# Transposes moved into the token loop, one engine per bank, and the guess products moved into the last pool of layer A

## The chip, the cores and the metric

The kernel runs on one core of one Trainium2 chip. The metric is the device time of the kernel in microseconds (us), as the median of several executions. Every execution has a profile summary with its span and the mean clock that the throttle granted to the matmul engine (PE).

Engine names in the profile: PE is the matmul engine, PEld its weight loads, DVE the vector engine, ACT the scalar engine, POOL the third elementwise engine, SP the engine that issues most DMAs. A transpose is a PE product with the identity. Products are written to a buffer called PSUM; a "bank" is one of its parts, and a "pool" is the kernel's reservation of tiles in it.

## The reference, cut to what matters

```python
x = A_x                                    # (1, 2048, 640), bf16
x = x + A(layernorm(x))                    # A: rfft2, times W, irfft2
x = x + B(layernorm(x), mem0, Wq, Wk, Wv, Wo)
x = x + A(layernorm(x))
x = x + B(layernorm(x), mem0, Wq, Wk, Wv, Wo)

def B(x, mem, ...):                        # 64 segments of 32 tokens, 32 heads of 128
    for s in range(64):
        h = concat(mem, x[segment s])      # 8 memory rows, then 32 tokens
        q, k, v = h @ Wq, h @ Wk, h @ Wv
        o = softmax(mask(q @ k.T * scale)) @ v @ Wo
        mem, out = o[:8], o[8:]
```

The recurrence over `mem` is not run segment by segment. The kernel guesses all memories at once from the segments' mean rows (mean rows times `Wv`, then times `Wo`), computes all segments in parallel, and checks the guess. That guess is what "guess products" means below.

The passage from A to B occurs twice. There, the last step of A yields normalized rows with tokens on the partitions, and B needs them transposed, with features on the partitions (`hT`), before its first query (q), key (k) and value products.

## The kernel before

The last step of layer A is a loop over 16 row tiles of 128 rows. `spectrum_d` and `tokens` are 6 + 6 products for a tile. `norm` normalizes two tiles. `add_u` adds a tile's rows to the segment sums.

```python
# Layer A, tokens(): the end of A
with tc.manual_schedule(engines={PE, ACT, DVE}):          # order as written
    for s0 in range(16 + 5):
        if s0 < 16:
            spectrum_d(s0)                 # psg, copied to Gs by ACT
        if 1 <= s0 <= 16:
            tokens(s0 - 1)                 # psy, copied to x by ACT, statistics on DVE
        if s0 >= 2 and s0 % 2 == 1 and s0 < 18:
            norm((s0 - 3) // 2)            # Ln, Exp on ACT; 4 tiny ops and 2 scalings on DVE
        if handoff is not None:
            if s0 < 10:
                handoff.wv_piece(s0)       # DMA of Wv
            if s0 >= 5:
                handoff.add_u(pp, xna[:, s0 - 5, :], s0 - 5)   # 5 small products
if handoff is not None:
    handoff.finish(pp)                     # segment means u
pp.release()                               # the last PSUM pool of A ends
if handoff is not None:
    handoff.transpose_all(xna)

# BStart.transpose_all: 80 transposes, in PSUM pools of their own
for c in range(5):
    ps = pt.tile([128, 16, 128], BF16, name="pstr", tag="pstr")     # two banks
    for s0 in range(16):
        nc.tensor.transpose(out=ps[:, s0, :], in_=xna[:, s0, c * 128:(c + 1) * 128], identity=ident[:])
    for g_ in range(4):
        dst = ...                          # 480 columns of hT
        src = ps[:, :, 2 * GS * g_:2 * GS * (g_ + 1)].rearrange("p s (w j) -> p w j s", j=2)
        (nc.vector.tensor_copy if g_ % 2 == 0 else nc.scalar.copy)(out=dst, in_=src)
    ...                                    # four smaller copies, also on both engines

# layer B, head 0, in PSUM pool pj
guess[0](pj, vb)                           # 160 products of 64 columns: Wv times u
q_x(w, 0)
q_x(w, 1)
guess[1](pj, vb)                           # 160 more: through Wo; cast; scatter into hT
...                                        # then the k products, which read those columns
```

## Time and profile before

| | before |
|---|---|
| median of 4 runs | 1654.55 us (1652.97 to 1655.66) |
| profiled span, mean granted PE clock | 1658.3 us, 0.987 |
| PE busy | 1563.1 us, 94% |
| first q product after the loop's start, passage 1 / 2 | 56.0 / 56.0 us |
| first k product after the loop's start, passage 1 / 2 | 72.3 / 72.3 us |

These are from the page of the kernel before: the busy time of each engine, and the chain of waits that ended last, by engine. PE is nearly always busy, and the work that follows one piece on the other is PE's.

```profile
PE 1563.1 (94%) x14240; PEld 1081.0 (65%) x14241; DVE 790.0 (48%) x2300; ACT 835.6 (50%) x2528; POOL 282.4 (17%) x206
...
PE 41%; DVE 2%; DMA 2%; ACT 1%; issue 0%; SPq 0%; DVEq 0%; ACTq 0%
```

So there is little to gain on average, but the passage is not average. This is the view by stretches of the kernel before, for the loop, the tail up to the first q product, and the two q heads with the second guess. The columns are the stretch (from:to), its length, then the busy time of PE, PEld, DVE, ACT and POOL with their instructions in brackets, the granted PE clock, the DMA share and GB/s.

```profile
94.00:122.90 28.90, 28.68 (x257) 20.57 (x256) 23.02 (x79) 23.40 (x44) 1.46 (x2) 1.00 0.91 321
122.90:150.00 27.10, 15.56 (x266) 14.86 (x267) 13.23 (x51) 10.29 (x30) 0.00 (x0) 0.75 0.40 120
150.00:166.30 16.30, 14.87 (x235) 10.16 (x232) 0.95 (x5) 5.62 (x13) 0.00 (x0) 1.00 0.01 2
```

The loop is PE-bound (28.68 of 28.90). The tail is not: PE works 15.56 of 27.10 us, and at a mean clock of 0.75. This is PE's timeline of that tail. The columns are start, duration, engine, line, operation, output<-input, shapes and count; in square brackets stands how long PE had been idle before, and for whom. Consecutive equal instructions are one line.

```profile
124.88 0.68 PE L1191 MATMUL psu<-sel,A1tok_S 128*128 128x64 bf16 x10 [2.20 <-DVE A1tok_S L120]
128.11 0.81 PE L1191 MATMUL psu<-sel,A1tok_S 128*128 128x64 bf16 x10 [2.55 <-DVE A1tok_S L120]
129.90 0.27 PE L1200 MATMUL psm<-ident,m 8*128 8x8 bf16 x5 [0.98 <-ACT u L1231]
130.10 4.38 PE L1206 MATMUL pstr<-ident,A1tok_S 128*128 128x128 bf16 x48
136.98 3.47 PE L1206 MATMUL pstr<-ident,A1tok_S 128*128 128x128 bf16 x32 [2.49 <-DVE B1hT_S L1218]
143.94 6.20 PE L1248 MATMUL psvb<-u,B1wv_S 128*128 128x64 bf16 x160 [3.49 <-DVE B1hT_S L1218]
149.98 4.56 PE L865 MATMUL psq<-B1hT_S,bB_S 128*128 128x480 bf16 x25
...
159.99 5.29 PE L1255 MATMUL psg<-bB_S,Wo_sb 128*128 128x64 bf16 x160 [0.21 <-ACT bB_S L867]
166.32 0.37 PE L846 MATMUL psk<-B1hT_S,bB_S 128*128 128x502 bf16 x1 [1.04 <-DVE B1hT_S L1225]
```

Read it downwards. PE waits 2.20 and 2.55 us for the last normalized rows. It transposes 48 tiles, waits 2.49 us for a two-bank tile to be emptied, transposes 32 more, and waits 3.49 us for the last copies, because the guess products stand in a new pool that takes over those banks. Before the first k product it waits 1.04 us for the scattered guess.

The copies that it waits for are these; the timeline of DVE and ACT in the second passage, first tile.

```profile
944.42 0.66 DVE L1211 COPY B2hT_S<-pstr 128x480 bf16<-128x480 bf16 x1 [1.49 <-PE pstr L1206]
945.17 0.56 ACT L1211 COPY B2hT_S<-pstr 128x480 bf16<-128x480 bf16 x1 [2.81 <-DVE B2hT_S L1211]
```

ACT starts at 945.17, after DVE ended at 945.08, and its releaser is DVE's copy. Both read the same banks. The Trainium skill, page "PSUM — Partial Sum Buffer", section "PSUM bank collisions raise a hardware error", says why: two engines may not touch one bank (and quadrant of partitions) at the same time, reads included, so such accesses have to be ordered. The trace agrees: two engines together emptied a tile no faster than one after the other.

### The profile page before, as it was taken

To read this page: it belongs to the slowest core of one execution; us is meant where nothing else is said; L and a number is where in the kernel's file an instruction comes from. 1 tells how busy PE (TensorE), PEld (TensorE's weight loads), DVE (VectorE), ACT (ScalarE), POOL (GpSimd) and SP (SyncE) were. 2 spreads that over 40 slices of the span, in tenths; PEclk is the share of its full clock that TensorE was granted. 3 is DMA by queue.
4 is the path that set the end of the run, shared out by engine and by line. 5 is a ranking of instruction groups with operands and counts; after the bars stand their busy time and mean duration, and the time that the engine had idled before them with its cause. 6 is when DMAs were issued, how large, how long until landed. Compare 5 with 4: busy or idle time off the path is not lost. (4 is left out here: it accounts for less than half of the span.)

```text
span 1658.3 us, 36195 instructions
## 1 busy us (share of the span) xinstructions
PE 1563.1 (94%) x14240; PEld 1081.0 (65%) x14241; DVE 790.0 (48%) x2300; ACT 835.6 (50%) x2528; POOL 282.4 (17%) x206
## 2 busy tenths in 40 slices
PE   4887999999999999899988789999999999999998
PEld 2566666666666666677755666666666666666775
DVE  5772455555545554543356724545545454544110
ACT  5373566666666666511114636666666666663000
POOL 0810112121211111100026002121211111111000
PEclk9998999999999999999999899999999999999999
DMA  4472143434434343633302703434344343436241
GB/s 155 156 274 72 53 148 132 155 117 148 136 138 144 130 154 127 233 125 96 96 13 88 260 2 110 160 116 150 132 142 137 133 156 127 140 130 226 68 127 54
DMA packets 167873, 218.05 MB, mean 131 GB/s; under 512 B 7374, under 2 KB 141836, under 8 KB 159756
## 3 DMA queue, kind: packets, MB, share of 16 engines
q1 hardware_dynamic: 167084, 213.34, 38.5%
q8 instruction: 113, 1.85, 0.4%
q0 software_dynamic: 608, 2.30, 0.4%
q14 instruction: 68, 0.56, 0.1%
HBM read 170.52 MB, written 45.09 MB: 130 GB/s over the span
## 5 line engine op out<-in xcount | busy, mean ns | idle before, releaser
L846 PEld LDWEIGHTS <-bB_S 128*128 128x128 bf16 x3180 | 260.2, 97 | 185.9 <-issue 6.6
L990 DVE TENSOR_TENSOR bB_S<-pso,bB_S 128x480 bf16<-128x480 f32 (+1 forms) x320 | 189.4, 592 | 266.3 <-PE pso L981 249.4
L925 ACT ACTIVATE bB_S<-pss 128x269 bf16<-128x269 f32 (+5 forms) x576 | 213.3, 385 | 191.7 <-PE pss L922 177.2
L1140 PE MATMUL psx<-Wo_sb,bB_S 128*128 128x320 bf16 x2048 | 288.2, 299 | 3.9 <-DMA bB_S<-oTx_d 3.9
L1140 PEld LDWEIGHTS <-bB_S 128*128 128x128 bf16 x2048 | 197.2, 98 | 80.5 <-DMA bB_S<-oTx_d 4.6
L905 DVE CAST bB_S<-psk 128x495 bf16<-128x495 f32 (+3 forms) x320 | 191.3, 598 | 115.0 <-PE psk L846 84.8
L950 POOL TENSOR_TENSOR bB_S<-bB_S,bB_S 128x634 f32<-128x634 f32 x64 | 99.2, 1550 | 820.9 <-ACT bB_S L946 809.9
L926 DVE TENSOR_TENSOR bB_S<-bB_S,maskf 128x269 bf16<-128x269 bf16 (+5 forms) x576 | 162.9, 287 | 152.9 <-ACT bB_S L925 149.2
L914 ACT CAST bB_S<-psv 128x512 bf16<-128x512 f32 (+1 forms) x288 | 160.5, 557 | 83.8 <-PE psv L912 83.4
L890 ACT ACTIVATE bB_S<-psq 128x480 bf16<-128x480 f32 x300 | 152.5, 508 | 97.9 <-PE psq L846 97.9
L846 PE MATMUL psk<-B2hT_S,bB_S 128*128 128x495 bf16 (+3 forms) x800 | 165.0, 342 | 2.6 <-DVE bB_S L905 1.4
L846 PE MATMUL psk<-B1hT_S,bB_S 128*128 128x495 bf16 (+3 forms) x800 | 165.0, 342 | 1.7 <-DVE B1hT_S L1225 1.2
L912 PE MATMUL psv<-bB_S,B1hT_S 128*128 128x256 bf16 x1360 | 163.4, 272 | 0.2 <-DVE bB_S L905 0.2
L912 PE MATMUL psv<-bB_S,B2hT_S 128*128 128x256 bf16 x1360 | 163.4, 272 | 0.2 <-DVE bB_S L905 0.2
L922 PEld LDWEIGHTS <-bB_S 128*128 128x128 bf16 x1216 | 103.1, 98 | 90.1 <-issue 6.3
L846 PE MATMUL psq<-B2hT_S,bB_S 128*128 128x495 bf16 (+5 forms) x780 | 157.6, 336 | 0.1
L846 PE MATMUL psq<-B1hT_S,bB_S 128*128 128x495 bf16 (+5 forms) x780 | 157.5, 336 | 0.1
L922 PE MATMUL pss<-bB_S 128*128 128x132 bf16 (+8 forms) x1216 | 148.4, 216 | 3.0
L912 PEld LDWEIGHTS <-B1hT_S 128*128 128x128 bf16 x1360 | 128.7, 98 | 13.7 <-issue 0.3
L912 PEld LDWEIGHTS <-B2hT_S 128*128 128x128 bf16 x1360 | 128.6, 98 | 13.7 <-issue 0.3
L981 PE MATMUL pso<-bB_S,bB_S 128*128 128x132 bf16 (+8 forms) x1216 | 119.6, 216 | 0.0
L981 PEld LDWEIGHTS <-bB_S 128*128 128x128 bf16 x1216 | 91.2, 98 | 15.7 <-DVE oTmf L991 0.5
(225 smaller groups left out, 1555.1 us busy)
## 6 DMA issues: line engine op xcount, KB each, us to landing
bB_S<-Rd SPq DMA_DIRECT2D x62, 1059.5 KB
oTx_d<-bB_S SPq DMA_DIRECT2D x60, 512.0 KB
bB_S<-oTx_d SPq DMA_DIRECT2D x56, 512.0 KB
bB_S<-in_B_Wq_dram SPq DMA_DIRECT2D x32, 320.0 KB
bB_S<-in_B_Wk_dram SPq DMA_DIRECT2D x32, 320.0 KB
bB_S<-in_B_Wv_dram SPq DMA_DIRECT2D x32, 320.0 KB
bB_S<-oTx_d SPq DMA_DIRECT2D x14, 384.0 KB
Wo_sb<-in_B_Wo_dram SPq DMA_DIRECT2D x4, 1280.0 KB
```

The lines of the kernel that those rows point to most:

```text
L846: nc.tensor.matmul(ps, lhsT=w[:, ch, hh * 128:(hh + 1) * 128], rhs=src[:, ch, lo:hi], start=(ch == 0), stop=(ch == 4))
L890: nc.scalar.mul(out=qv[:, :, 0:SEG], in_=x_view(ps, o, n)[:, :, 1:SW], mul=scale)
L905: nc.vector.tensor_copy(out=KTs[h % 2][:, lo:hi], in_=ps[:, 0:hi - lo])
L912: nc.tensor.matmul(ps[:, i * 256:(i + 1) * 256], lhsT=hT[:, ch, (t + i) * 128:(t + i + 1) * 128], rhs=w["Wv"][:, ch, :], start=(ch == 0), ...
L914: nc.scalar.copy(out=V[:, t:t + n, :].rearrange("p a b -> p (a b)"), in_=ps[:, 0:n * 256])
L922: nc.tensor.matmul(ps[:, off - o0:off - o0 + hi - lo], lhsT=KT[:, t * 128:(t + 1) * 128], rhs=QT[:, lo:hi], start=True, stop=True)
L925: nc.scalar.activation(out=E[:, 0:n], in_=ps[:, 0:n], func=ACTF.Exp)
L926: nc.vector.tensor_tensor(out=P[:, o0:o0 + n], in0=E[:, 0:n], in1=bs.mask[:, o0:o0 + n], op=ALU.mult)
L950: nc.gpsimd.tensor_tensor(out=accS, in0=accS, in1=sums_sb, op=ALU.add)
L981: nc.tensor.matmul(pso[:, lo - q0:hi - q0], lhsT=V[:, t, (h % 2) * 128:(h % 2 + 1) * 128], rhs=P[:, off:off + hi - lo], start=(i == 0), st ...
L990: nc.vector.tensor_tensor(out=oT.rearrange("p (r s j) -> p r s j", r=16, j=2)[:, :, s0:s0 + ns, :], in0=byclass(po), in1=rx, op=ALU.mult)
L1140: self.tc.nc.tensor.matmul(ps[:, 0:320], lhsT=lhs(h, k // 2), rhs=self.g["Wo_sb"][:, h, c0:c0 + 320], start=(h == 0), stop=(h == H - 1))
```

## The change

Its intent: begin transposing while the loop still runs, in tiles of one bank each that a single engine empties, and fill the rest of the tail with fewer things to wait for.

- A transposed tile now holds two feature blocks of four row tiles (8 transposes, one bank). 48 of the 80 transposes stand in the loop, at iterations 8, 9, 10, 12, 13, 14 and 16; 32 stay in the tail.
- Each such bank is emptied by DVE or by ACT alone. For one copy to serve four groups of columns, the columns of `hT` get a uniform pitch of 512: the function `hcol` shifts columns from 512 on by 7, so the groups then start at odd columns (7, 519, ...).
- The small sum products leave the loop for the tail, where PE would wait.
- The four tiny operations of each norm go from DVE to POOL (in the loop).
- The first guess products run within the last pool of A; the second guess stands between the q products of heads 0 and 1.

The diff, cut to its core (helpers, renames and the split of the norm into two functions are left out):

```diff
         with tc.manual_schedule(...):
-            for s0 in range(16 + 5):
-                ...                                   # as shown above
-        if handoff is not None:
-            handoff.finish(pp)
+            moved, late = [], []
+            for i in range(16 + 1):
+                for f in moved:
+                    f()
+                moved = []
+                if late:
+                    late.pop(0)()
+                if i >= 5 and i % 2 == 1:
+                    norm((i - 5) // 2)                # now only the scalings, DVE
+                if i >= 2:
+                    stats(i - 2)
+                if i < 16:
+                    spectrum_d(i)
+                if 1 <= i <= 16:
+                    tokens(i - 1)
+                ...                                   # rest of late
+                if i >= 4 and i % 2 == 0:
+                    inverse((i - 4) // 2, nc.gpsimd)  # Ln, Exp on ACT; tiny ops on POOL
+                ...                                   # pieces of Wv, memory rows
+                if i >= 8 and i % 4 < 3:
+                    n = i % 4
+                    jobs = handoff.rows_out(handoff.rows_in(pp, xna, i // 4 - 2, 2 * n), n != 1 and i < 16)
+                    ...                               # jobs: the copies, done an iteration later
+            stats(15)
+            norm(6)
+            for s0 in range(14):
+                handoff.add_u(pp, xna[:, s0, :], s0)
+            big = handoff.big(pp)
+            inverse(7, nc.vector)
+            handoff.do(moved)
+            second = handoff.rows_in(pp, xna, 2, 2)
+            norm(7)
+            for s0 in (14, 15):
+                handoff.add_u(pp, xna[:, s0, :], s0)
+            handoff.finish(pp)
+            handoff.do(handoff.rows_out(second, False))
+            pairs = [handoff.rows_in(pp, xna, 3, 2 * n, ps=big[:, 2 * n:2 * n + 2]) for n in range(2)]
+            ones = [handoff.rows_in(pp, xna, q, 4) for q in (2, 3)]
+            for job, on_dve in ((pairs[0], True), (pairs[1], False), (ones[0], True), (ones[1], True)):
+                handoff.do(handoff.rows_out(job, on_dve))
+            handoff.guess1(pp)
         pp.release()
-        if handoff is not None:
-            handoff.transpose_all(xna)
 ...
+    def hcol(self, k):
+        return k + (self.PRE if k >= 512 else 0)      # PRE = 7
 ...
                 if h == 0:
-                    guess[0](pj, vb)
                     q_x(w, 0)
+                    env["guess"](pj, bs.vb)
                     q_x(w, 1)
-                    guess[1](pj, vb)
```

## The prediction

> **What bounds the kernel now.** The page gives PE 94% of the 1658.3 us span, 0.987 mean clock; the chain of waits is PE work in layer B (value, key, query and output products). The change leaves those alone. It touches the passage from layer A to B, which occurs twice (PE clock 0.73 there).
>
> From the timeline of the second passage (us):
> - 906.4 to 934.9: token loop. PE-bound: 12 matmuls make 1.65 per row tile, 1.80 once the five small sum products ride along. Engine table by stretches (907 to 935.5): PE 28.1 of 28.5, ACT 23.6, DVE 23.2.
> - 934.9 to 941.3: the last norms (two DVE statistics groups, two Ln/Exp, eight tiny DVE operations, four scalings); PE waits 2.2 + 2.6.
> - 941.3 to 956.3: 80 transposes (48 in 4.4, 32 in 3.5, at half clock) with waits of about 1.0, 2.5 and 3.5. Each bank pair is read by DVE (0.65) and ACT (0.56) alternately, and the timeline shows each starting only after the other ended. The Trainium skill's page "PSUM — Partial Sum Buffer", section "PSUM bank collisions raise a hardware error", explains the ordering: two engines may not touch one bank at once.
> - 956.3 to 962.4: guess products, 6.2.
> - 962.4 on: q products of heads 0 and 1 (5.0 each), guess products through Wo (5.3), then 1.0 to 1.2 idle until DVE's cast and scatter let the k products start.
>
> **What the change does, per passage.**
> Removed from the tail: 48 of 80 transposes and their evictions go into the loop; the alternation of engines ends; fewer copies per transpose (group pitch made uniform); the pool boundary between transposes and guess products disappears; four tiny DVE operations per norm go to POOL.
> Added to the loop: 48 transposes at full clock, 48 x 0.056 = 2.7; minus 11.5 sum-product groups of 0.15, -1.7. ACT gets 2 x 0.56 + about 0.2 at two iterations, DVE about 2.4 per four iterations: DVE then has about 8.4 against PE's 7.7 per four iterations, ACT about 7.5. So I expect lag and waits of PE for normalized rows or Gs copies: 1.5 to 2.5. Loop: +2.5 to +3.5.
> Tail, from the last token product: ACT copy 0.85, statistics 1.1, lag 0.7, norm(6) behind POOL 0.9, Ln/Exp and small operations 1.5, scaling 0.8 (PE resumes at about 5 instead of 6), sums and 24 transposes 2 to 3, guess products 5.3 to 6.2: q products start at about 14 instead of 27.4: -13.
> Second guess before q of head 1: cast and scatter hidden, -1.2.
> Net about -11 per passage (all estimates from the durations above), -22 in all. Practically all of it is on the critical path, since PE is idle or cold there.
>
> DMA is saturated (share about 0.95) until 946; weights of heads 0 and 1 land shortly after. I expect them in time.
> Odd column starts of hT: the trace already has odd-start weights and moving rows (back products in A) at 0.098 and full rate, so no loss.
>
> **Prediction:** 1632 us, range 1626 to 1639. Faster by over 2%: 4%; within 2%: 95%; slower: 1%.
>
> **Right if** the profile shows: first q product of each passage 10 to 12 us earlier relative to the loop's start; transposes at about 0.06 in the loop; loop 31 to 32.5 us long; k products following q of head 1 without the 1 us gap; layer B's middle unchanged to 1 us.
>
> **Wrong if** PE waits for DVE or POOL inside the loop much longer (slow tiny POOL operations delay norms; gain shrinks by 3 to 6); the first weights land late because the queue is shared with stores; weight loads from odd columns slow (2720 of them); or the tail overlaps better than summed (gain to 28).

## The result, and the profile after

| | before | after |
|---|---|---|
| median of 4 runs | 1654.55 us | 1635.12 us (1632.62 to 1636.59) |
| ratio, with its 95% interval | | 0.9882 (0.9865 to 0.9899) |
| profiled span, granted clock | 1658.3 us, 0.987 | 1632.3 us, 0.994 |
| first q product after the loop's start | 56.0 / 56.0 us | 44.8 / 45.6 us |
| first k product after the loop's start | 72.3 / 72.3 us | 59.5 / 60.2 us |

A ratio is always the mean time of one kernel's runs over that of the other's of the same rounds, so it is not quite the ratio of the medians quoted. The interval says that the change is faster by 1.0 to 1.4%. All outputs are right.

The page of the kernel after: the same number of products, POOL with 70 more instructions, DVE with 58 fewer.

```profile
PE 1556.5 (95%) x14240; PEld 1071.8 (66%) x14241; DVE 780.6 (48%) x2242; ACT 837.0 (51%) x2520; POOL 294.8 (18%) x276
```

The stretches of the first passage of the kernel after, as before: loop, tail, the two q heads with the second guess.

```profile
93.60:124.20 30.60, 29.92 (x239) 21.16 (x238) 21.40 (x62) 25.86 (x50) 7.09 (x32) 1.00 0.84 302
124.20:138.50 14.30, 10.71 (x284) 9.72 (x285) 9.66 (x39) 8.89 (x21) 1.00 (x5) 1.00 0.77 232
138.50:153.10 14.60, 14.18 (x230) 9.60 (x230) 1.48 (x6) 4.86 (x12) 0.00 (x0) 1.00 0.01 2
```

The loop is 1.7 us longer: PE works 1.24 more and is idle 0.68 instead of 0.22. The tail is 12.8 shorter, and its clock is 1.00 instead of 0.75. The last stretch is 1.7 shorter. In the tail PE's idle time fell from 11.5 us (27.10 - 15.56) to 3.6 (14.30 - 10.71), and its busy time by 4.9.

PE's timeline of the kernel after: one batch of eight transposes inside the loop, then the end of the loop and the tail.

```profile
107.99 0.61 PE L1291 MATMUL pstr<-ident,A1tok_S 128*128 128x128 bf16 x8
108.44 1.00 PE L412 MATMUL psg<-A1gt_S,A1UT_S 128*128 128x321 bf16 x6
...
124.69 0.81 PE L1291 MATMUL pstr<-ident,A1tok_S 128*128 128x128 bf16 x6 [0.49 <-DVE A1tok_S L127]
125.64 1.92 PE L1254 MATMUL psu<-sel,A1tok_S 128*128 128x64 bf16 x60
128.38 0.68 PE L1254 MATMUL psu<-sel,A1tok_S 128*128 128x64 bf16 x10 [0.82 <-DVE A1tok_S L127]
...
130.48 1.06 PE L1291 MATMUL pstrb<-ident,A1tok_S 128*128 128x128 bf16 x16
...
132.69 0.38 PE L1291 MATMUL pstr<-ident,A1tok_S 128*128 128x128 bf16 x4 [0.93 <-ACT B1hT_S L1310]
132.91 4.87 PE L1274 MATMUL psvb<-u,B1wv_S 128*128 128x64 bf16 x160
138.46 4.54 PE L931 MATMUL psq<-B1hT_S,bB_S 128*128 128x480 bf16 x25 [0.67 <-ACT bB_S L1276]
143.45 4.83 PE L1338 MATMUL psg<-bB_S,Wo_sb 128*128 128x64 bf16 x160 [0.21 <-ACT bB_S L933]
...
153.10 4.66 PE L912 MATMUL psk<-B1hT_S,bB_S 128*128 128x502 bf16 x25 [0.21 <-ACT bB_S L933]
```

In the loop eight transposes took 0.45 us (107.99 to 108.44), 0.056 each; in the tail before, at a mean granted clock of 0.63 (half clock but for the last 1.1 us), 48 took 4.4 us, 0.09 each. Where PE waited 2.55 us for rows it now runs the 60 postponed sums and then waits 0.82. The guess products follow the last transpose without a wait (3.49 before), and k follows q after 0.21 (1.04 before).

The copies now overlap, because they read different banks; the timeline of DVE and ACT in the loop of the kernel after.

```profile
118.39 1.32 DVE L1306 COPY B1hT_S<-pstr 128x480 bf16<-128x480 bf16 x2
...
119.23 0.77 ACT L1306 COPY B1hT_S<-pstr 128x480 bf16<-128x480 bf16 x1
```

DVE's two copies last from 118.39 to 119.71 and ACT's begins at 119.23.

Outside the passage one group changed. These are the 495-column k products of the first layer B, of the kernel before and of the kernel after, in the view of groups by form (busy us and mean ns of one after the bar).

```profile
L846 PE MATMUL psk<-B1hT_S,bB_S 128*128 128x495 bf16 x320 | 75.9, 372 | 0.0
```

```profile
L912 PE MATMUL psk<-B1hT_S,bB_S 128*128 128x495 bf16 x320 | 76.2, 373 | 0.0
```

One nanosecond each is little, but there are some 2500 products of this kind. From the first to the last of the heads' stores that the trace lets one time (the stores `Rd<-bB_S`, the first to the fourth from the end), layer B took 458.72 us before and 459.61 after in the first layer, and 459.92 and 461.01 in the second: 0.9 and 1.1 us were given back (1.0 and 0.8 between the first and the last store `oTx_d<-bB_S`).

**The sum.** In the profiles the passages give -12.8 and -12.1 (loop's start to first k), the heads +2.0, and the way from the first k to the first store -0.3 each: -23.5 us. The median of the first pairing says -19.4 and the profiled spans say -26.0. The experiments below say which is nearer.

### The profile page after: what moved, and what is told of

The parts are those of the page before. It is cut to its first block, busy times and chain, and to the rows that moved or that the text cites. A ratio compares the mean times of both kernels' runs of the same rounds, so it can differ in the third digit from the quotient of the medians.

```text
span 1632.3 us, 36236 instructions
## 1 busy us (share of the span) xinstructions
PE 1556.5 (95%) x14240; PEld 1071.8 (66%) x14241; DVE 780.6 (48%) x2242; ACT 837.0 (51%) x2520; POOL 294.8 (18%) x276
## 3 DMA queue, kind: packets, MB, share of 16 engines
q1 hardware_dynamic: 167084, 213.34, 39.1%
```

## The experiments

Two calls of four kernels (e7, e2, e3, e4; then e0, e1, e5, e8), one of three (e6, e9, e10) and one of e11 alone, each call on one chip together with the kernel before; compare within a call where a few tenths of a per cent matter. "Mean" is the mean of the runs of those rounds.

| run | what | median us | ratio to before (95%) | mean, before in the same rounds |
|---|---|---|---|---|
| e7_before_again | the kernel before, again | 1656.39 | 0.9992 (0.9978 to 1.0005) | 1656.64 for before |
| e2_swap_only | before, second guess earlier | 1654.1 | 0.9988 (0.9974 to 1.0001) | 1654.64, 1656.64 |
| e3_one_engine | before, one engine per tile | 1649.64 | 0.9965 (0.9951 to 0.9978) | 1650.4, 1656.64 |
| e4_all_in_tail | after, no transposes in the loop | 1648.98 | 0.9949 (0.9936 to 0.9963) | 1649.12, 1656.64 |
| e0_after_again | the kernel after, again | 1633.16 | 0.9856 (0.9836 to 0.9876) | 1633.22, 1656.25 |
| e1_even | after, even columns | 1631.18 | 0.9851 (0.9836 to 0.9866) | 1631.4, 1656.25 |
| e5_inverse_dve | after, tiny operations on DVE | 1635.67 | 0.9877 (0.9862 to 0.9892) | 1635.95, 1656.25 |
| e8_even_u_late | e1, one copy before the means | 1630.53 | 0.9842 (0.9828 to 0.9855) | 1630.25, 1656.25 |
| e6_guess_outside | after, first guess in B's pool | 1636.73 | 0.9881 (0.9863 to 0.99) | 1636.19, 1655.87 |
| e9_stats_first | after, statistics before scaling | 1629.76 | 0.9846 (0.9827 to 0.9866) | 1630.32, 1655.87 |
| e10_best | e8 and e9 and two last tiles | 1629.5 | 0.984 (0.982 to 0.986) | 1629.28, 1655.87 |
| e11_even_stats_first | e1 and e9 | 1629.06 | 0.9849 (0.9826 to 0.9872) | 1629.76, 1655.38 |

And in the traces, from the start of the token loop to the start of the last transpose (passage 1) and of the first q and k products (passage 1 / 2):

| run | last transpose | first q | first k |
|---|---|---|---|
| before | 46.2 | 56.0 / 56.0 | 72.3 / 72.3 |
| e7_before_again | 46.0 | 56.6 / 55.6 | 73.0 / 72.0 |
| e2_swap_only | 46.1 | 55.8 / 55.7 | 71.0 / 70.8 |
| e3_one_engine | 43.3 | 52.1 / 52.2 | 68.5 / 68.6 |
| e4_all_in_tail | 47.0 | 53.5 / 53.2 | 68.2 / 67.8 |
| after | 39.2 | 44.8 / 45.6 | 59.5 / 60.2 |
| e0_after_again | 39.2 | 44.8 / 46.6 | 59.5 / 62.7 |
| e1_even | 39.3 | 45.0 / 45.9 | 59.7 / 60.6 |
| e5_inverse_dve | 40.5 | 46.1 / 46.3 | 60.7 / 61.0 |
| e6_guess_outside | 39.2 | 46.3 / 47.8 | 60.9 / 62.5 |
| e8_even_u_late | 38.4 | 45.0 / 46.3 | 59.7 / 60.9 |
| e9_stats_first | 38.5 | 44.1 / 45.0 | 58.8 / 59.7 |
| e10_best | 38.5 | 44.7 / 44.7 | 59.4 / 59.4 |
| e11_even_stats_first | 39.1 | 44.8 / 45.7 | 59.5 / 60.4 |

### How far do equal kernels differ? e7_before_again and e0_after_again

No edit: the kernel before and the kernel after, again.

> Control: the kernel before, unchanged, against itself. The profiled spans of before and after differ by 26.0 us, the medians of the runs by 19.4. Theory: the first profiled run of before (1660 us) was a run with some us more of cold clock or waits than usual, and this one shows a span near 1653 to 1656 us and a ratio of 1.000 within 0.2%. Rival: the passages really gain 25 us and something else loses 5; then this span is 1658 to 1660 again.

> Control for the next three: the kernel after, unchanged, on their chip. Expected 1633 to 1637 us, ratio 0.987 to 0.990, and pairs of heads in layer B 32.86 us apart as in its first profile (before: 32.80).

The kernel before against itself gave 0.9992, with 1 inside the interval. Its five spans were 1657.8, 1654.6, 1651.9, 1653.4 and 1654.8 us at granted clocks of 0.987, 0.990, 0.990, 0.989 and 0.989. The kernel after gave 1633.4, 1634.7, 1628.3 and 1629.4 at 0.995, 0.994, 0.998 and 0.998. The longer runs are those with the lower clock, so a single run is uncertain by some 3 us either way, and the three estimates of the gain (19.4, 23.0 here by the means, 26.0 by the profiles) do not contradict each other. The sum of 23.5 from the landmarks agrees with the 23.0. Single landmarks scatter too. Equal kernels agree to 0.3 us at the last transpose, but in two traces of the kernel before the first q differs by up to 0.6, with stretches of half clock of different length, and in two traces of the kernel after, in the second passage, by 1.0 and the first k by 2.5. There a pause of PE of varying length stands before them (see "What stays open"). So the first passage and the last transpose are the better measures.

### Is it the place of the transposes or how they are emptied? e4_all_in_tail and e3_one_engine

The theory: most of the gain comes from the transposes' place in the loop, where PE does them at full clock while it is busy anyway. The rival: what counts is that two engines no longer take turns on a bank, wherever the transposes stand.

```diff
 # e4_all_in_tail, on the kernel after
-                if i >= 8 and i % 4 < 3:
+                if False:
 ...
-                second = handoff.rows_in(pp, xna, 2, 2)
 ...
-                handoff.do(handoff.rows_out(second, False))
+                n_job = 0
+                for q in range(3):
+                    for n in range(3):
+                        if (q, n) != (2, 2):
+                            handoff.do(handoff.rows_out(handoff.rows_in(pp, xna, q, 2 * n), n_job % 2 == 0))
+                            n_job += 1
```

```diff
 # e3_one_engine, on the kernel before (in transpose_all)
+                copy = nc.scalar.copy if c % 2 == 0 else nc.vector.tensor_copy
 ...
-                    (nc.vector.tensor_copy if g_ % 2 == 0 else nc.scalar.copy)(out=dst, in_=src)
+                    copy(out=dst, in_=src)
 ...                                        # the four smaller copies likewise
```

> The kernel after with its transposes of row tiles 0 to 11 taken out of the loop and put behind it, still four row tiles a bank, one engine a bank, DVE and ACT in turn. Theory (moving them under the loop is the main gain): loop shorter by 2.5 us (about 28), tail longer by about 8, so plus 5 us per passage and plus 10 us against the kernel after, about 1645 us (ratio to before about 0.994 to 0.995). Rival (one engine a bank and fewer copies are the main gain, the place is not): within 3 us of the kernel after (ratio 0.988 to 0.990).

> The kernel before with one edit: all copies of one transposed tile go to one engine (ACT for chunks 0, 2, 4, DVE for 1, 3), the place of the transposes unchanged after the loop. Theory (place matters most, the alternation of engines cost little): the last copy of a passage ends about 2.4 us earlier, from 13.9 us after the first transpose to about 11.5; minus 5 us in all (ratio 0.997). Rival (taking turns on a bank was the main cost): the copies run twice as dense, the last ends 5 us earlier or more, minus 10 us or more in all (ratio 0.994).

With everything in the tail, 1649.12 us: 7.5 of the gain are left, and some 15.5 of the 23.0 are gone (the means, each against the kernel before; against the 19.4 of the first pairing, some 12). In the trace the first q is 8.7 and 7.6 us later than in the kernel after. The theory had put the loss at about 10 us: right in kind and too small. PE's timeline of e4 shows what the tail then does; this is a part of it.

```profile
127.68 1.90 PE L1295 MATMUL pstr<-ident,A1tok_S 128*128 128x128 bf16 x16
130.46 0.61 PE L1295 MATMUL pstr<-ident,A1tok_S 128*128 128x128 bf16 x4 [0.89 <-DVE B1hT_S L1314]
131.29 1.86 PE L1295 MATMUL pstr<-ident,A1tok_S 128*128 128x128 bf16 x16 [0.22 <-ACT B1hT_S L1314]
134.01 0.59 PE L1295 MATMUL pstr<-ident,A1tok_S 128*128 128x128 bf16 x4 [0.86 <-ACT B1hT_S L1314]
```

The granted clock is 0.50 throughout the 12 us from 127 to 139. Sixteen transposes take 1.9 us, 0.12 each with the end of the last, instead of 0.056, and PE waits for a bank to come free after each batch. Also, e4's loop gives back only part: its last `psy` product starts 28.2 us after the loop's start against 30.2 in the kernel after, although 48 transposes of 0.056 are 2.7 us. It is 28.2 in the kernel before too, with the sum products still in the loop.

What e4 does not separate: it keeps the two one-bank tiles of the kernel after, so the waits for a bank (0.89, 0.22, 0.86 and 0.91 us in the first passage) are part of its loss. No run had all transposes in the tail with more banks.

One engine per tile by itself was worth 6.2 us of means, 3.9 and 3.7 at the first q of the two passages: less than the rival's figure of about 10, a little more than the theory's of about 5. ACT's and DVE's copies of e3, from its timeline, with the transposes that they let through:

```profile
128.11 5.39 PE L1207 MATMUL pstr<-ident,A1tok_S 128*128 128x128 bf16 x64
...
130.09 1.95 ACT L1212 COPY B1hT_S<-pstr 128x480 bf16<-128x480 bf16 x4 [2.12 <-PE pstr L1207]
...
131.63 2.35 DVE L1212 COPY B1hT_S<-pstr 128x480 bf16<-128x480 bf16 x4 [3.08 <-PE pstr L1207]
```

The two engines now work side by side on different tiles, four copies back to back in 1.95 and 2.35 us, and 64 instead of 48 transposes pass without a wait. So the rival is a real part, the smaller one: up to the first k, the gain from before to e4 (which also has the other parts) is 4.1 and 4.5 us per passage, that from e4 to after 8.7 and 7.6. The parts do not simply add: at the first q e3 alone gains more (3.9 and 3.7) than e4 with one engine per bank and the rest (2.5 and 2.8).

### The second guess by itself: e2_swap_only

```diff
 # on the kernel before
                     q_x(w, 0)
-                    q_x(w, 1)
                     guess[1](pj, vb)
+                    q_x(w, 1)
```

> The kernel before with one edit: the guess products through Wo stand between the q products of heads 0 and 1. Theory (the cast and the scatter of the guess, 1.5 us, hide behind the q products of head 1): minus 1.2 us in each passage, minus 2.4 us in all (ratio 0.9985), and the wait of the first k product for the scatter (1.0 us) gone in the profile. Rival (the swap is worth nothing by itself since PE then waits elsewhere, for the cast of the guess or for the first keys): ratio 1.000.

The first k came 1.3 and 1.5 us earlier in the trace, the first q only 0.1 and 0.3; from the one to the other it is 1.2 less in both passages. The time fell by 2.0 us of means, with 1 still inside the interval, so it is the trace that shows the effect, and the time only agrees.

### The pool boundary by itself: e6_guess_outside

```diff
 # on the kernel after
-                handoff.guess1(pp)
         pp.release()
 ...
                 if h == 0:
+                    bs.guess1(pj)             # the first guess again in B's own pool
                     q_x(w, 0)
```

> The kernel after with the guess products through Wv moved out of the last pool of layer A into layer B's own pool, as they were before; the order of the products on PE is unchanged. Theory (a new pool waits for the last copies of the old one): the guess products start when the last copy of a transposed bank ends, about 2.3 us later than now (39.3 us after the loop's start now, 41.5 then), and the wait of 0.7 us of the first q product goes: plus 1.5 to 2.5 us per passage, plus 3 to 5 us against the kernel after. Rival (the boundary only changes place): within 1 us in all.

PE's timeline of e6 where the first guess begins, which in the kernel after had no wait:

```profile
133.88 4.83 PE L1273 MATMUL psvb<-u,B1wv_S 128*128 128x64 bf16 x160 [2.18 <-ACT B1hT_S L1312]
```

The wait for the last copy is back, 2.18 us; in return the 0.67 before the q products is gone, for that was the same boundary in another place. Net 1.5 us at the first q of the first passage, and in the second 2.2 against the kernel after or 1.2 against e0. The time alone does not show it: the ratio is 0.9881, in another call than e0 with 0.9856 (about 4 us), and the kernel after had 0.9882 in its first pairing.

### The tiny operations of the norm on POOL: e5_inverse_dve

```diff
 # on the kernel after
-                    inverse((i - 4) // 2, nc.gpsimd)
+                    inverse((i - 4) // 2, nc.vector)
```

> The kernel after with the five tiny operations of each norm in the loop on DVE (four there) and not on POOL. Theory A (my prediction's: DVE is the fuller engine at 8.4 us of work per 7.7 us of PE work, so POOL's help matters): DVE lags by 0.75 us per norm at the end, plus 0.5 to 2 us per passage. Rival B (POOL's chain of 1.5 us and two hand-overs is on the way to the normalized rows, PE waits 0.5 us for them after the loop, so DVE is as good): within 0.5 us per passage either way, or shorter.

On DVE again, the last transpose comes 1.2 us later in both passages, the first q 1.2 and 0.7, and the means differ by 2.7 us in the same rounds. The rows arrive later: in the second passage of e5, PE waits 1.49 us after the first 60 sums, where the kernel after waits 0.82. (In the first passage of e5 the 60 sums ran at half clock, which hid part of that wait.)

```profile
924.84 0.67 PE L1254 MATMUL psu<-sel,A2tok_S 128*128 128x64 bf16 x10 [1.49 <-DVE A2tok_S L127]
```

The prediction feared that slow POOL operations would delay the norms. In the loop POOL took about 0.20 us for each of its 30 tiny operations (the other two of the 32 are fills, 1.19 us together), and it was DVE that had little time to spare.

### The odd columns: e1_even

```diff
 # on the kernel after
-        return k + (self.PRE if k >= 512 else 0)
+        return k + (self.PRE + 1 if k >= 512 else 1)
 ...                                        # memory rows to columns 1 to 8, groups from PRE + 1
```

The first run of 502 columns now starts at column 1, and all 495-column runs start at even columns.

> The kernel after with one more column in front of hT, so that the four wide groups start at columns 8, 520, 1032, 1544 (even) and not 7, 519, 1031, 1543. Theory (moving rows that start at an odd bf16 column cost a product about 1 ns more: 495-wide k products are 373 ns after, 372 before, heads 0.033 us further apart): the pairs of heads return to 32.80 us, minus 1.6 to 2 us in all against the kernel after. Rival (the 0.033 us come from another cause, such as the queue or where the buffers lie): pairs stay at 32.86 us.

The group of 495-column k products in e1:

```profile
L912 PE MATMUL psk<-B1hT_S,bB_S 128*128 128x495 bf16 x320 | 75.9, 372 | 0.0
```

It is back at the 75.9 us of the kernel before, and the period of two heads fell from 32.867 us to 32.813 (32.800 before). The rest, 0.013, goes with the 502-column products, now the odd ones: 39.2 us for 160 instead of 39.0, 375 ns each instead of 374. Over 32 pairs of heads in both layers 0.054 is 1.7 us; the means of the same rounds say 1.8. The intervals of the two kernels overlap, so the time alone would not show it, but the same product changing with the parity of its column in both directions does.

### Looking for a better version: e8, e9, e10, e11

```diff
 # e8_even_u_late: e1, and
-                handoff.finish(pp)
                 handoff.do(handoff.rows_out(second, False))
+                handoff.finish(pp)
```

```diff
 # e9_stats_first: on the kernel after
-                if i >= 5 and i % 2 == 1:
-                    norm((i - 5) // 2)
                 if i >= 2:
                     stats(i - 2)
+                if i >= 5 and i % 2 == 1:
+                    norm((i - 5) // 2)
```

```diff
 # e10_best: e8 and e9, and the last two pairs in two PSUM tiles
-        return pp.tile([128, 4, 4, 128], BF16, name="pstrb", tag="pg", bufs=3)
+        return [pp.tile([128, 4, 4, 128], BF16, name="pstrb", tag="pg", bufs=3) for _ in range(2)]
```

`e11_even_stats_first` is e1 with e9.

> e1_even with one more edit: ACT empties the second transposed pair before it scales the sums u, and not after. The last group of four transposes waits 0.93 us for that emptying. Theory: that wait goes to nearly nothing and the guess products start 0.4 to 0.9 us earlier, so minus 1 to 2 us against e1_even and minus 3 to 4 us against the kernel after. Rival: u comes too late and PE waits the same time for it; equal to e1_even.

> The kernel after with one edit: in the loop DVE computes the statistics of the newest row tile before it scales the pair that waits for POOL, and not after. Theory (loop held by a ring: DVE scaling waits for POOL, POOL for ACT's Ln and Exp, ACT for DVE's statistics that stand behind the scaling): the loop gets 0.5 to 1 us shorter (last token product 29.2 to 29.7 us after the loop's start, not 30.2), minus 1 to 2 us in all. Rival (the loop is held by PE's own work and by ACT's two visits to transposed banks): loop unchanged, and the rows come later, so equal or up to 1 us per passage slower.

> All together: even columns, statistics first, the second pair emptied before u, and the last two pairs in two PSUM tiles and not in one, so that DVE and ACT empty them at the same time (in the kernel after ACT waits 0.86 us there for DVE). Theory: guess products start 38.4 or less after the loop's start and run without the 0.8 us wait seen in e8_even_u_late, first q product at 43.5 to 44.3 us in the first passage; minus 5 to 8 us against the kernel after (ratio to before 0.980 to 0.983). Rival (PE waits for its own instructions or for the clock there, whatever the copies do): equal to e8_even_u_late, ratio 0.984.

> The kernel after with the two edits that each helped alone and did not meet the half clock: even columns and statistics first. Theory (e10_best gave nothing more because the queue of small products behind the loop ran at half clock in its first passage, after PE had waited 0.83 us for rows and had little work before): without the two other edits the first q product comes at 44.1 to 44.3 us in the first passage as in e9_stats_first, heads 32.81 us per pair, about 1628 to 1629 us, ratio 0.983. Rival (what is left is noise of the clock): 1629 to 1631, like e8, e9 and e10.

e8 brought the last transpose and the first guess 0.8 us forward, as intended, and the q products not at all. PE's timeline of its second passage says why:

```profile
930.02 2.00 PE L1274 MATMUL psvb<-u,B2wv_S 128*128 128x64 bf16 x63 [0.81 <-ACT B2hT_S L1313]
...
933.09 0.66 PE L1274 MATMUL psvb<-u,B2wv_S 128*128 128x64 bf16 x17 [1.06 <-issue]
```

The guess now waits 0.81 us within its products, for the bank that ACT empties last, and there is a pause of 1.06 us that no semaphore explains (below).

e9 left the loop as long as it was (last `psy` product at 30.2 us in both passages), so the theory that statistics placed late lengthen the loop fell. But the tail became 0.7 us shorter, since the rows before the last were ready earlier: 70 sums go in one piece, where the kernel after has 60, a wait and 10.

e10 and e11 should have added these up. They did not: e10 came out as its rival had it, equal to e8. In part the cause is in the clock: e10's last transpose stands at 38.5 us in the first passage, which met the half clock, and at 37.7 in the second, which did not. This is e10's view by stretches, and after it the sums in e10's timeline.

```profile
124.00:126.00 2.00, 1.05 (x13) 0.60 (x12) 1.32 (x4) 1.17 (x4) 0.86 (x5) 1.00 0.13 39
126.00:128.00 2.00, 2.00 (x44) 1.98 (x45) 1.93 (x7) 0.37 (x2) 0.39 (x2) 0.59 1.04 349
```

```profile
126.13 3.74 PE L1254 MATMUL psu<-sel,A1tok_S 128*128 128x64 bf16 x70
```

Seventy sums took 3.74 us, where e9 needs 2.42 for the same seventy: PE was granted 0.59 of its clock just then. In e11 they took 3.75, at 0.50 and 0.65, and its second passage met the half clock too. For e11 the rival, that the noise of the clock would hide the gain, was the right one.

e8 to e11 have medians from 1629.06 to 1630.53, some 3 us under the kernel after at best; e8 against it in the same rounds is 1630.25 to 1633.22, a ratio of 0.998. Their intervals overlap with each other's and with that of e0, so they beat the kernel before clearly, by 1.5 to 1.6%, and no one of them is shown to beat another.

## Why the prediction was right or wrong

The predicted time of 1632 us (1626 to 1639) held: 1635.12 and, again, 1633.16. The sum had these terms per passage.

| term, as predicted | predicted | measured (profiles) | verdict |
|---|---|---|---|
| loop | +2.5 to +3.5 | +1.7 | too large |
| tail to first q | -13 | -12.8 / -12.1 | right |
| second guess hidden | -1.2 | -1.7 | a little too small |
| layer B's middle, odd columns "no loss" | 0 | +0.9 / +1.1 per layer | wrong |
| net per passage | about -11 | -11.5 (half of 23.0) to -11.8 (half of 23.5) | right |

Part of the exactness is luck, since errors of opposite sign met: for both passages together the loop (2.6 against the middle of its range) and the second guess (1.0) came out better than reckoned, the tail (1.1) and the odd columns (2.0) worse.

- **What bounds the kernel: right.** The passages gained 24.9 us on the way to the first k products, and 23.0 arrived in the mean time.
- **The tail: right, for the reasons given.** The wait before the second group of transposes, the wait at the pool boundary and half a clock are gone. e4 shows that the place in the loop is the larger part (8.7 and 7.6 us of 12.8 and 12.1, waits for its two banks included), e3 that one engine per bank is a smaller one, e6 that the boundary is 1.2 to 2.2. Two parts of the change no run tried alone: the move of the sum products to the tail, and the uniform pitch with its fewer copies.
- **The loop: mis-sized.** The step was "I expect lag and waits of PE for normalized rows or Gs copies: 1.5 to 2.5", and the loop should have been "31 to 32.5" long. It was 30.6. The products came out as reckoned (0.056 us a transpose; PE's busy time rose by 1.24), but the new idle time was 0.46, not 1.5 to 2.5. The wait was of the kind expected, for a Gs copy of ACT, but it came once in the loop, 0.53 us:

```profile
123.38 0.30 PE L423 MATMUL psy<-A1tok_S,A1gt_S 128*128 128x320 bf16 x1 [0.53 <-ACT A1tok_S L413]
```

  The term that was off is DVE's load: "about 8.4 against PE's 7.7 per four iterations". This is a stretch of four iterations of the kernel after with transposes in them, in the view by stretches, and below it the same stretch of e5, where DVE also has the tiny operations.

```profile
108.80:116.40 7.60, 7.57 (x62) 5.25 (x60) 6.75 (x21) 7.09 (x16) 2.00 (x10) 1.00 0.96 354
```

```profile
108.80:116.40 7.60, 7.29 (x64) 5.13 (x61) 7.36 (x24) 6.46 (x13) 0.00 (x0) 1.00 0.92 333
```

  DVE was busy for 6.75 us, ACT for 7.09, PE for 7.57: nobody was tighter than PE in this stretch, and PE was idle for only 0.03 of it. With the tiny operations on DVE it comes to 7.36 and PE falls to 7.29 of 7.60.
- **The second guess: right.** The wait for the scatter fell from 1.04 to 0.21. e2, the swap alone in the kernel before, takes 1.2 off the way from the first q to the first k, as predicted. The other 0.5 of the 1.7 is the guess itself, 4.83 us instead of 5.29 (it took 5.29 in e2 too); why it got shorter was not looked into.
- **Odd columns: the wrong step.** "Odd column starts of hT: ... full rate, so no loss" was taken from wide groups in layer A whose parity had not been compared with anything. e1 shows a loss of 1 ns for each 495-column product, and 1.7 to 1.8 us in the whole program came back. The Trainium skill, page "SBUF — State Buffer", section "Operand start alignment", allows any start on an element and says that this "is about legality, not speed": it promises nothing about the time. The claim "layer B's middle unchanged to 1 us" was thus met only at its limit: 0.9 and 1.1 us by one pair of stores, 1.0 and 0.8 by the other.
- **The full clock: expected at the transposes, larger in effect than reckoned.** The Trainium skill, page "TensorE: Matmul & The Clock Gate", section "Part 1: The HAM clock gate", says that the clock is whole or half (a third state needs three busy cores), and is set from how busy PE was in windows of about 3.4 us. The traces agree: the granted clock is only ever 1.0 or 0.5 and changes in steps of 3.41 us, and the mean of the tail rose from 0.75 to 1.00. That is one reason why e4 lost 15 us and not 10: its transposes are at half clock again (0.12 us each). PE was busy for 2.31 and 1.64 us in the windows from 128.90 and 132.32, and the clock stayed at half; it rose after the window from 135.73, in which PE was busy throughout, with transposes almost alone.

**What stays open.** In the second passage PE pauses near the end of the first guess products, in most of the runs that have them there, after product 143 of 160 (144 in e10): for 0.59 us in the kernel after, 1.68 in e0, 0.74 in e1, 1.06 in e8, and 0.57 to 0.71 in e9, e10 and e11, but not in e4 and e5. No semaphore is waited for; the profile calls it "issue".

```profile
935.42 0.66 PE L1274 MATMUL psvb<-u,B2wv_S 128*128 128x64 bf16 x17 [1.68 <-issue]
936.75 6.00 PE L931 MATMUL psq<-B2hT_S,bB_S 128*128 128x480 bf16 x25 [0.67 <-ACT bB_S L1276]
```

These two lines are e0's timeline. After the pause and the wait the clock fell to half, and the 25 q products took 6.00 us instead of 4.5. In these seven traces a packet of the queue for instructions, of 16 KB, ended 1.28 to 1.53 us before PE went on (in the kernel after it was underway from 934.10 to 935.26, and PE resumed at 936.66). The Trainium skill, page "Runtime: NRT & Kernel Launch", section "Instruction fetch mechanics", says that instructions come in blocks of 16 KB over a queue of their own and that crossing a block is "mostly hidden". The size agrees; the pause would then be a place where it is not hidden, behind a DMA that was nearly full until shortly before (until about 934.6 in the kernel after). This is a coincidence in time in seven traces. No run moved the fetch or emptied the queue, so it is not shown.

Also open is how much of the remaining 3.6 us of idle PE in the tail can be had: e8 to e11 removed some waits and got others, or a half clock, in return.

## What to carry to other kernels

When two engines empty one PSUM tile, give each its own bank: they then work side by side instead of in turns, and PE waits less. Better still, move such transposes into a PE-bound stretch of the loop before, where they cost 0.056 us each at full clock, instead of a tail where PE waits, the clock falls to half, and a transpose costs nearly twice as much (0.12 in e4). When a layout is shifted to make copies simpler, count the products that read it afterwards: a nanosecond on each of thousands of them gave back 2 of 25 us.

## What the Trainium skill lacked or had wrong

- "SBUF — State Buffer", section "Operand start alignment", gives no cost for PE when moving rows of bf16 start at an odd column, and no other page that was consulted does. The runs show about 1 ns for each product of 495 columns (372 to 373 ns; 75.9 to 76.2 us for 320), and 0.067 us for each pair of heads.
- "TensorE: Matmul & The Clock Gate", section "Part 1: The HAM clock gate", puts the fall to half clock after an idle window. In e10 it fell to half at 126.36, though PE had been busy 1.88 of the 3.41 us before (0.55), and in e11 at 123.97 after the same share. The page says that the window runs free; each trace gives its phase, by the times at which the clock changes. Cut into windows in this way, the fourteen traces show a fall after windows with PE busy for up to 0.60 and never above, and a full clock kept after windows down to 0.43 and never below. In between both occur (in e9 it stayed full after 1.94 of 3.41, 0.57, from 916.87 on), so the profile's busy share alone does not decide, and the page gives no share.
- "Runtime: NRT & Kernel Launch", section "Instruction fetch mechanics", calls a fetch of 16 KB mostly hidden. Pauses of PE of 0.57 to 1.68 us followed such packets, which came at the end of a stretch with the DMA nearly full; the cause is not shown.
- No page that was consulted gives the time of a copy out of PSUM by the length of its runs. 480 elements a partition took 0.562 us on ACT and 0.652 on DVE with runs of 16 elements in the output, and 0.754 and 0.716 with runs of four, which also have one more dimension. Which of the two counts was not separated.
- No page that was consulted gives the time of a tiny POOL operation. On 128 partitions of two fp32 elements it took about 0.20 us (2.00 us for the ten between 108.80 and 116.40).
